# Attention and two expert layers on one core: k's low part in one subtract, rank work behind the last products

## The chip, the cores and the metric

One core of a Trainium2 chip. Times are device microseconds of the whole kernel; lower is better. TensorE (PE in the rows), VectorE (DVE), ScalarE (ACT), GpSimd (POOL) and SyncE (SP, which only issues DMAs) each run their own queue of instructions in order and wait for each other by semaphores.

## The reference

Causal attention with 4 batches of 12 heads, 448 tokens and 64 columns a head, then two mixture-of-experts layers over the 1792 tokens of 768 columns:

```python
scores = scale * np.matmul(q, k.transpose(0, 1, 3, 2))
scores = np.where(mask, -1000000000.0, scores)
attn = softmax(scores)
x = np.matmul(attn, v)
logits = x @ w_gate + modality_bias[modality_id]
e_idx = np.argmax(logits, axis=1)
h = np.maximum(x[mask] @ w1[e], 0.0)
out[mask] = gate_w[mask, None] * (h @ w2[e])
```

The lines on logits, experts and output run twice: the first layer (m1 below) with a modality bias on the logits, the second (m2) without, on the output of the first. There are 8 experts, each with w1 of 768x1024 and w2 of 1024x768. A token goes to one expert.

## The kernel before, in words

Every float32 matrix is split in a high part (type fp32r) and a low part (the rest), and a product is made of three: high by high, high by low, low by high. In m1 the names are `h` and `l` for a weight's high and low part, `xh` and `xl` for the tokens, `hth` and `htl` for the hidden rows. High parts are made by ScalarE (L765 for weights), low parts by VectorE (L769).

**Attention** works on 24 pairs of heads. The string ORDER (L37 to L46) lists the steps of one body, each with an offset that says of which pair; bodies overlap, so one body holds steps of several pairs. `trans` transposes q or k on PE into PSUM, `thi` makes the high part on ScalarE, `tlo` (L113 to L125) the low part on VectorE. Two heads sit in the 128 partitions, 64 each. From pair 1 on a score is two matmuls (L165, L166): the first has q's high and low part of one head stacked in 128 rows against k's high part twice (moved there by DMAs, `mv`), the second k's low part against q's high part. So that the second counts one head alone, k's low part goes into `klz`, a pair of buffers of 128 x 2 x 448 whose other half is zero from the start (L260 to L263): two subtracts, one for each head (L125). `score` (L146 to L166) is in the printed code below.

At each `step` of ORDER the loop over the plan (L300 to L325) pops one function from a list `todo`: the routing of a batch, once the batch's heads are done (`Route1.stages`, L499 to L614; `batch`, L1150). Batch 2, the third, is routed between the heads of the fourth; PW, PL and XW (L328) count empty steps in it. Then m1's first tokens are gathered and transposed. `turn` (L1062) turns the gate's weights for m2 by six transposes into the bank `turned`, two copies to `y` and a DMA, at the head of body 1. WARM (L33) is the count of matmuls on zeros at the start.

**The expert layers** work in blocks of 128 tokens of one expert. `Moe.body` (L950 to L1013) is one block: up products (L832 to L835), the hidden rows to ScalarE, transposes (`htrans`, L858 to L866, which makes `hth` on ScalarE and `htl` on VectorE), down products (L844) into two halves `py[0]` and `py[1]` of 384 columns, each over the first four (KA) and the second four (KB) slices of 128 hidden rows, and the scaling (L881). In `down` a list names the products: "hh" is `h` by `hth`, "lh" is `h` by `htl`, "hl" is `l` by `hth`; those in one list alternate slice by slice. `switch` (L900) loads and splits the next expert's weights where the next block has another. Most blocks run in a device loop (L943 to L948); the one before it is of kind "first", the ones behind it "before" and "last". At the loop's head and end the engines meet.

While m1 runs, the next layer's routing is done for the block before: eight logits of a block on VectorE (L1253, from `y` by `wgb`), `choose` (L671 to L679), `ranks` (L697 and L698 on PE, L699 and L702 on ScalarE) and `rows` (L706 to L725 on VectorE). These hang on hooks of the block: head1 (L1262), up21 (L1269), choose, down1. m2 has the same body without them.

Of the kernel before, what the change touches and what calls it, by code (L numbers as in the profile page):

```python
# [22 lines left out]
E = 8  # L23
FF = 1024
CP = 112
# [7 lines left out]
WARM = 12  # L33
SLOW = 5
# [9 lines left out]
    expo_1_3:1 step expo_1_2:0 thi_q:-1 step ocopy_1:2 ptrans_1_0:1 plo_0_2:1 step score_0_3:0 phi_1_0:1 expo_1_0:0 step  # L44
# [5 lines left out]
def attention(tc, cst, q, k, v, wg1, x1, lg, psh, spare, hooks):  # L50
# [6 lines left out]
    with ExitStack() as c:  # L57
# [54 lines left out]
        def tlo(n, nm):  # L112
            pt, x = pair[n]["pt" + nm], pair[n]["x" + nm]  # L113
            if nm == "q":
                if n == 0:
                    lo = pair[n]["ql"] = spare[:, :S]
                else:
                    lo = pair[n]["ql"] = qk.tile([128, S], F32R, tag="ql", name=f"ql{n}", bufs=1)
                nc.vector.scalar_tensor_tensor(out=lo, in0=pt, scalar=-0.125, in1=x[:, 0], op0=ALU.mult, op1=ALU.subtract)
            else:  # L120

                lo = pair[n]["kl"] = klz[n % 2]
                for j in range(2):
                    r = slice(j * HD, (j + 1) * HD)
                    nc.vector.tensor_tensor(out=lo[r, j], in0=pt[r], in1=x[r, 0], op=ALU.subtract)  # L125
# [16 lines left out]
        def score(n, j, i):  # L142
            s = unit.setdefault((n, j), {})
            r = slice(j * HD, (j + 1) * HD)
            xq, xk, kl = (pair[n][x] for x in ("xq", "xk", "kl"))
            w = (i + 1) * CP  # L146

            o = CP if i == 1 else 0
            key = f"bank{max(i, 1)}"
            if key not in s:  # L150

                sp, tag = [(ps_s, "ps"), (psh, "h0"), (psh, "h1")][scores[0] % 3]
                scores[0] += 1
                s[key] = sp.tile([CP, max(w, 3 * CP)], F32, tag=tag, name=f"ps{n}_{j}_{i}", padded_shape=[CP, 512])
            bank = s[key]
            ps = s["ps", i] = bank[:, o : o + w]
            qs = slice(i * CP, w)
            if n == 0:

                ql = pair[n]["ql"]  # L160
                nc.tensor.matmul(ps, xq[r, 0, qs], xk[r, 0, :w], start=True, stop=False)
                nc.tensor.matmul(ps, ql[r, qs], xk[r, 0, :w], start=False, stop=False)
                nc.tensor.matmul(ps, xq[r, 0, qs], kl[r, j, :w], start=False, stop=True)  # L163
            else:
                nc.tensor.matmul(ps, xq[:, j, qs], xk[:, j, :w], start=True, stop=False)  # L165
                nc.tensor.matmul(ps, xq[:, j, qs], kl[:, j, :w], start=False, stop=True)  # L166
# [50 lines left out]
        def ocopy(n, j):  # L217

            t = unit[n, j]["t"] = sm.tile([128, S], F32, tag="t", name=f"t{n}_{j}", bufs=3)
            nc.scalar.copy(t, unit[n, j]["o"])  # L220
# [16 lines left out]
        def norm(n, g):  # L237
# [4 lines left out]
            l = get(ll, b, sm, [CP, NC, H, E], tag="ll", name=f"ll{b}", bufs=2)  # L242
# [17 lines left out]
        klz = [one.tile([128, 2, S], F32R, name=f"klz{i}") for i in range(2)]  # L260
        for x in klz:
# [4 lines left out]
        for _ in range(WARM):  # L266
            nc.tensor.matmul(warm, idle[:, :128], idle[:, :512], start=True, stop=True)
# [13 lines left out]
        steps = dict(load=load, mv=mv, store=store, splitv=splitv, trans=trans, thi=thi, tlo=tlo, score=score, mini=mini, expo=expo, ptrans=ptrans, phi=phi,  # L281
# [27 lines left out]
        for at, (body, f, n) in enumerate(plan):  # L309
            if body == 1 and plan[at - 1][0] < 1:  # L310
                hooks["turn"](ps_o.tile([128, 512], F32, tag="po", name="turned"))
# [16 lines left out]
PW, PL, XW = 12, 4, 24  # L328
# [149 lines left out]
class Route1:  # L478
# [17 lines left out]
    def stages(self, b, bias, first):  # L496
# [120 lines left out]
        return choice + [self.wait] + rank + slot[:2] + gate[:2] + slot[2:4] + gate[2:4] + slot[4:6] + gate[4:] + slot[6:] + rest  # L617
# [159 lines left out]
class Moe:  # L777
# [173 lines left out]
    def body(self, j, hooks, kind=""):  # L951
# [40 lines left out]
        down(py, 0, KA, ["hh", "lh"])  # L992
# [8 lines left out]
        down(py, 0, KA, ["hl"])  # L1001
        if last:
            down(py, 1, KA, ["hh", "lh"])
# [22 lines left out]
def tile_attention_moe_moe(ctx: ExitStack, tc, q, k, v, mid, wg1, bias, w1a, w2a, wg2, w1b, w2b, out):  # L1026
# [31 lines left out]
    with tc.tile_pool(name="bias", bufs=1) as p:  # L1058
# [3 lines left out]
        def turn(bank):  # L1062

            src = st["hs"][:, : KD * E].rearrange("p (k e) -> p k e", e=E)
            for a, b in ((0, 4), (4, KD)):
# [3 lines left out]
            nc.sync.dma_start(wgt, y[:E])  # L1069
# [192 lines left out]
    def head1(j):  # L1262
        out1(j)
        logits(0, 1, 2, 3, 4, 5)
# [6 lines left out]
    def up21(j):  # L1271
        r2.slots()
        logits(6, 7)
# [25 lines left out]
    with tc.manual_schedule():  # L1299
# [143 lines left out]
```

## Time and profile before

| | |
|---|---|
| median of 3 runs | 953.6 us (952.13 to 954.86) |
| profiled execution | 953.22 us |
| its span in the profile | 950.1 us |
| attention, by the trace | to some 262 us |
| m1's loop | 302.4 to 537.1 us |
| mean granted clock of PE | 0.99 of 2.4 GHz |

The page gives the busy time of each engine, the waits of an engine name who ended them, and the timeline lists the instructions of a stretch, with the idle time before them in brackets. Windows give the busy time of each engine in a stretch and the clock that PE was granted. All times of rows are counted from the start of the span.

### The profile page before, as it was taken

What the parts mean: (1) busy time and instruction counts of PE and PEld (TensorE: products, weight loads), DVE (VectorE), ACT (ScalarE), POOL (GpSimd) and SP (SyncE); (2) the same over time, 40 slices, a digit from 0 to 9 for tenths busy, and PEclk for the clock granted to TensorE, in tenths of its full rate; (3) what the DMA queues carried; (4) which work ended last, traced back from release to release, by engine and by line L of the source; (5) the groups of instructions that cost most, each with busy time, mean ns of one, the idle gap of its engine ahead of it and who ended that gap; (6) DMA issues with size and microseconds to landing.
All of it is one profiled execution on the core that took longest, in us unless ns stands there. A gap on an engine that the chain in (4) does not pass through costs nothing. (4 is left out here: it accounts for less than half of the span.)

```text
span 950.1 us, 21195 instructions
## 1 busy us (share of the span) xinstructions
PE 907.9 (96%) x5432; PEld 804.2 (85%) x5433; DVE 626.6 (66%) x1792; ACT 494.1 (52%) x1137; POOL 170.5 (18%) x225
## 2 busy tenths in 40 slices
PE   7999999999999999988999999999999999999996
PEld 5898898988768898877998788788888888988885
DVE  4999999998566766798767688511176117383743
ACT  4998888888552222271222277212276226573653
POOL 5122414228310000000000000111012102030202
PEclk8999999999999999998999999999999999999999
DMA  6777887766367121245112043540069116295610
GB/s 139 167 184 174 191 194 189 181 167 163 140 219 290 50 66 50 72 166 199 55 61 77 18 171 146 196 171 30 36 227 360 49 33 247 92 344 220 243 48 8
DMA packets 121721, 138.50 MB, mean 146 GB/s; under 512 B 77175, under 2 KB 96759, under 8 KB 121350
## 3 DMA queue, kind: packets, MB, share of 16 engines
q1 hardware_dynamic: 116902, 118.23, 40.9%
q0 software_dynamic: 4768, 19.67, 6.1%
q8 instruction: 22, 0.36, 0.2%
q14 instruction: 29, 0.24, 0.1%
HBM read 117.69 MB, written 24.01 MB: 149 GB/s over the span
## 5 line engine op out<-in xcount | busy, mean ns | idle before, releaser
L769 DVE TENSOR_TENSOR l<-raw,h 128x768 fp32r<-128x768 f32 (+1 forms) x148 | 147.5, 1061 | 12.1 <-ACT h L765 11.9
L765 ACT CAST h<-raw 128x768 fp32r<-128x768 f32 (+1 forms) x154 | 131.2, 925 | 7.5 <-issue 5.4
L866 DVE SCALAR_TENSOR_TENSOR htl<-m2ht,hth 128x512 fp32r<-128x512 f32 x36 | 24.8, 690 | 143.1 <-ACT hth L865 143.1
L1253 DVE CUSTOM_DVE_ANT_0 junk<-y,wgb 128x768 bf16<-128x768 f32 x104 | 99.5, 957 | 14.2 <-ACTq L900 8.6
L178 ACT ACTIVATE P<-ps,m 112x336 f32<-112x336 f32 (+1 forms) x192 | 95.4, 505 | 22.2 <-DVE m L171 21.4
L844 PE MATMUL m2y<-h,hth 128*128 128x384 f32 x272 | 93.1, 342 | 0.0
L171 DVE CUSTOM_DVE_ANT_0 ps<-ps,mask 112x336 f32<-112x336 f32 (+1 forms) x192 | 85.5, 456 | 10.7 <-PE ps L163 4.2
L844 PE MATMUL m2y<-h,htl 128*128 128x384 f32 x272 | 91.6, 337 | 0.0
L832 PE MATMUL m2h<-h,xh 128*128 128x512 f32 x204 | 81.9, 402 | 1.2 <-ACTq L947 1.2
L207 DVE TENSOR_TENSOR ptl<-pp,pth 112x448 fp32r<-112x448 f32 x144 | 77.7, 540 | 6.3 <-ACT pth L201 6.1
L833 PE MATMUL m2h<-h,xl 128*128 128x512 f32 x204 | 80.9, 396 | 0.0
L194 PE MATMUL pp<-cident,P 112*112 112x112 f32 x480 | 71.3, 263 | 5.8 <-DVE ptl L207 5.4
L201 ACT CAST pth<-pp 112x448 fp32r<-112x448 f32 x144 | 67.2, 480 | 10.0 <-PE pp L194 9.5
L844 PE MATMUL m1y<-h,htl 128*128 128x384 f32 x192 | 65.8, 343 | 5.3 <-DVE htl L866 5.3
L844 PE MATMUL m1y<-h,hth 128*128 128x384 f32 x192 | 67.5, 351 | 0.0
L194 PEld LDWEIGHTS pp<-cident,P 112*112 112x112 f32 x480 | 52.0, 134 | 15.5 <-PE ps L166 6.1
L795 POOL DMA_INDIRECT xg<-y_scratch,ic x21 | 21.4, 1018 | 232.4 <-PE m2y L844 148.5
L214 PE MATMUL po<-pth,vs 112*128 112x448 f32 x192 | 62.2, 337 | 0.0
L844 PE MATMUL m2y<-l,hth 128*128 128x384 f32 x272 | 60.3, 343 | 1.1 <-issue 0.4
L165 PE MATMUL ps<-xk,xq 128*112 128x336 f32 (+3 forms) x184 | 60.6, 337 | 0.4 <-ACT P L178 0.2
L795 POOL DMA_INDIRECT xg<-x_scratch,ic x16 | 16.4, 1023 | 248.2 <-PE m1y L844 195.5
L1189 POOL DMA_INDIRECT out_dram<-y,ic x19 | 36.4, 1915 | 124.6 <-ACTq L900 66.4
(459 smaller groups left out, 2192.6 us busy)
## 6 DMA issues: line engine op xcount, KB each, us to landing
raw<-in_moe_w_dram SPq DMA_DIRECT2D x46, 1536.0 KB, 9.7
xk<-xk SPq DMA_DIRECT2D x69, 112.0 KB, 3.5
y_scratch<-y SPq DMA_DIRECT2D x16, 384.0 KB
lk<-in_k_dram SPq DMA_DIRECT2D x48, 112.0 KB, 2.6
lq<-in_q_dram SPq DMA_DIRECT2D x48, 112.0 KB, 3.3
lv<-in_v_dram SPq DMA_DIRECT2D x24, 224.0 KB, 4.5
x_scratch<-xs SPq DMA_DIRECT2D x24, 224.0 KB, 3.0
xq<-ql SPq DMA_DIRECT2D x46, 112.0 KB, 2.7
```

The costliest lines, as they stand in the source:

```text
L171: nc.vector.tensor_tensor_reduce(out=s["ps", i], in0=s["ps", i], in1=mask[:, S - (i + 1) * CP :], scale=1.0, scalar=3.0e38, op0=ALU.add, o ...
L178: nc.scalar.activation(P, s["ps", i], AF.Exp, bias=s["m"][:, i : i + 1], scale=-1.0, accum_out=rs[:, j, i : i + 1])
L194: nc.tensor.transpose(pt[:, at : at + CP], s["P", i][:, kc * CP : (kc + 1) * CP], ident[:CP, :CP])
L201: nc.scalar.copy(h[:, a : a + w], pt)
L207: nc.vector.tensor_tensor(out=l[:, a : a + w], in0=pt, in1=s["pth"][:, a : a + w], op=ALU.subtract)
L214: nc.tensor.matmul(o[:, kc * CP :], vs[:, j, kc, :], s["pth"][:, seg], start=kc == 0, stop=False)
L765: self.nc.scalar.copy(hi[k], raw[:, k, :])
L769: eng.tensor_tensor(out=lo[k], in0=raw[:, k, :], in1=hi[k], op=ALU.subtract)
L832: mm(ph, xh[:, s], W.h1[k][:, f], start=k == 0, stop=False)
L833: mm(ph, xl[:, s], W.h1[k][:, f], start=False, stop=False)
L844: mm(py[n], rows[p[0]][:, s], (W.h2 if p[1] == "h" else W.l2)[k][:, f], start=k == 0 and p == "hh", stop=stop and k == ks[-1] and p == par ...
L1253: vec.tensor_tensor_reduce(out=junk, in0=y, in1=wgb[:, e], scale=1.0, scalar=0.0, op0=ALU.mult, op1=ALU.add, accum_out=r2.lg[:, e : e + 1])
```

## The change

It has five parts.

1. k's low part is one subtract of 128x448 into a plain tile `kl`. The zero-padded pair of buffers is now q's (`qz`): a new step `alone`, after q's high part, copies it there on GpSimd, one copy of 64x448 for each head, from pair 1 on. The second matmul of a score is `kl` by `qz`.
2. The tiles `t` of `ocopy` have two buffers in place of three, `ll` one in place of two.
3. Three more matmuls on zeros (FILLS) come ahead of the transposes of k of pair 1. `turn` is in two parts: four transposes and a copy where all was before, the last two, their copy and the DMA at the 12th step of body 1.
4. PL is 8 in place of 4, XW 28 in place of 24, and three empty steps (RW) in place of one stand ahead of the ranks of batch 2.
5. In blocks of all kinds but "last" the down products go KA high rows, KA low rows, KB high rows, KB low rows, for both halves; the hook "down" with ranks and rows comes behind the two scales. Of the logits three come in head1 and five after `htl` of the first half; in the block before the last two (`upy`) three of them come after the choice of the likeliest expert.

```diff
+FILLS = 3
+TURN = 12
...
-    expo_1_3:1 step expo_1_2:0 thi_q:-1 step ocopy_1:2 ptrans_1_0:1 plo_0_2:1 step score_0_3:0 phi_1_0:1 expo_1_0:0 step
+    expo_1_3:1 step expo_1_2:0 thi_q:-1 alone:-1 step ocopy_1:2 ptrans_1_0:1 plo_0_2:1 step score_0_3:0 phi_1_0:1 expo_1_0:0 step
...
-
-                lo = pair[n]["kl"] = klz[n % 2]
+                lo = pair[n]["kl"] = qk.tile([128, S], F32R, tag="kl", name=f"kl{n}")
+                nc.vector.tensor_tensor(out=lo, in0=pt, in1=x[:, 0], op=ALU.subtract)
+
+        def alone(n):
+
+            if n > 0:
                 for j in range(2):
                     r = slice(j * HD, (j + 1) * HD)
-                    nc.vector.tensor_tensor(out=lo[r, j], in0=pt[r], in1=x[r, 0], op=ALU.subtract)
+                    nc.gpsimd.tensor_copy(qz[n % 2][r, j], pair[n]["xq"][r, 0])
...
-                nc.tensor.matmul(ps, xq[:, j, qs], kl[:, j, :w], start=False, stop=True)
+                nc.tensor.matmul(ps, qz[n % 2][:, j, qs], kl[:, :w], start=False, stop=True)
...
             if body == 1 and plan[at - 1][0] < 1:
-                hooks["turn"](ps_o.tile([128, 512], F32, tag="po", name="turned"))
+                turns = hooks["turn"](ps_o.tile([128, 512], F32, tag="po", name="turned"))
+                turns.pop(0)()
+            elif body == 1 and f == "step" and turns and sum(p[:2] == (1, "step") for p in plan[:at]) == TURN:
+                turns.pop(0)()
+            elif (f, n) == ("trans_k", 1):
+
+                warmth(FILLS)
...
-PW, PL, XW = 12, 4, 24
+PW, PL, RW, XW = 12, 8, 3, 28
...
-        return choice + [self.wait] + rank + slot[:2] + gate[:2] + slot[2:4] + gate[2:4] + slot[4:6] + gate[4:] + slot[6:] + rest
+        return choice + [self.wait] * (RW if b == B - 2 else 1) + rank + slot[:2] + gate[:2] + slot[2:4] + gate[2:4] + slot[4:6] + gate[4:] + slot[6:] + rest
...
-        down(py, 0, KA, ["hh", "lh"])
+
+        down(py, 0, KA, ["hh", "lh"] if last else ["hh", "hl"])
...
-            down(py, 1, KA, ["hh", "lh"])
-            down(py, 1, KA, ["hl"])
-            down(py, 0, KB, ["hh", "lh"])
-            down(py, 0, KB, ["hl"], True)
-            hook("down")
-            down(py, 1, KB, ["hh", "lh"])
-            down(py, 1, KB, ["hl"], True)
+            down(py, 1, KA, ["hh", "hl"])
+            down(py, 0, KA, ["lh"])
+            down(py, 1, KA, ["lh"])
+            down(py, 0, KB, ["hh", "hl"])
+            down(py, 1, KB, ["hh", "hl"])
+            down(py, 0, KB, ["lh"], True)
+            down(py, 1, KB, ["lh"], True)
         for n in range(2):
             self.scale(py, col, n)
+        if not last:
+            hook("down")
...
     def head1(j):
         out1(j)
-        logits(0, 1, 2, 3, 4, 5)
+        logits(0, 1, 2)
...
         r2.slots()
-        logits(6, 7)
+        logits(3, 4, 5, 6, 7)
...
-            logits(6, 7)
+            logits(3, 4)
             r2.most(count("cntz", r2.ohs))
             edv["s"], edv["e"], edv["a"] = r2.e0(ET.SP), r2.e0(ET.DVE), r2.e0(ET.Activation)
+            logits(5, 6, 7)
```

ScalarE at the end of a block of m1's loop, before: the copy of the ranks and the exponential (L699, L702) stand ahead of the two scales (L881).

```order
L699 COPY r2rk<-rk_5289 128x8
L702 REGISTER_ALU
L702 ACTIVATE r2ex,r2se<-r2d 128x8
L881 ISA
L881 ACTIVATE y<-m1y_5104,t1gate 128x384
L881 REGISTER_ALU
L881 ACTIVATE y<-m1y_5105,t1gate 128x384
```

The same with the change:

```order
L897 ISA
L897 ACTIVATE y<-m1y_5150,t1gate 128x384
L897 REGISTER_ALU
L897 ACTIVATE y<-m1y_5151,t1gate 128x384
L715 REGISTER_ALU
L715 COPY r2rk<-rk_5352 128x8
L718 REGISTER_ALU
L718 ACTIVATE r2ex,r2se<-r2d 128x8
```

Copy and exponential now come behind both scales, and the row work on VectorE waits for that copy.

PE at the same place, before: the ranks (`rk`) stand between the first half's last low weights and the second half's twelve KB products, of which the first stand here.

```order
L844 MATMUL m1y_5104<-l_6_4569,hth 128x384
L844 MATMUL m1y_5104<-l_7_4570,hth 128x384
L697 REGISTER_ALU
L697 LDWEIGHTS cones
L697 MATMUL rk_5289<-r2ohs,cones 128x8
L698 REGISTER_ALU
L698 LDWEIGHTS ctri
L698 MATMUL rk_5289<-r2oh,ctri 128x8
L844 MATMUL m1y_5105<-h_4_4559,hth 128x384
L844 MATMUL m1y_5105<-h_4_4559,htl 128x384
```

With the change (m1y_5150 is the first half, m1y_5151 the second):

```order
L860 MATMUL m1y_5151<-h_6_4610,htl 128x384
L860 MATMUL m1y_5151<-h_7_4611,htl 128x384
L713 REGISTER_ALU
L713 LDWEIGHTS cones
L713 MATMUL rk_5352<-r2ohs,cones 128x8
L714 REGISTER_ALU
L714 LDWEIGHTS ctri
L714 MATMUL rk_5352<-r2oh,ctri 128x8
L916 COMPARE_AND_BRANCH
```

The ranks are the block's last matmuls, and the products with `htl` stand just before them.

VectorE in the loop body around `htl` of the first half, before; each logit is an instruction on 128x768 and a read of its sum:

```order
L1253 ISA junk,r2lg<-y,wgb 128x768
L1253 ISA r2lg 128x1
L866 REGISTER_ALU
L866 SCALAR_TENSOR_TENSOR htl<-m1ht_5133,hth 128x512
L1253 REGISTER_ALU
```

With the change, from the third logit to the second one behind `htl`:

```order
L1276 ISA junk,r2lg<-y,wgb 128x768
L1276 ISA r2lg 128x1
L882 REGISTER_ALU
L882 SCALAR_TENSOR_TENSOR htl<-m1ht_5179,hth 128x512
L1276 REGISTER_ALU
L1276 ISA junk,r2lg<-y,wgb 128x768
L1276 ISA r2lg 128x1
```

Before, six logits stand ahead of `htl` and two behind it; with the change three and five. Behind the last logit come, in both, the low parts of the second half of W2 (where the expert changes), the tokens' low parts, `htl` of the second half and `choose`.

## Rows read from the trace of the kernel before

**Rows 1.** The page: span, and busy us (share) xinstructions of each engine.

```profile
span 950.1 us, 21195 instructions
...
PE 907.9 (96%) x5432; PEld 804.2 (85%) x5433; DVE 626.6 (66%) x1792; ACT 494.1 (52%) x1137; POOL 170.5 (18%) x225
```

**Rows 2.** List of waits of PE: waiting line <- who ended it: us, times, longest.

```profile
PE pp L194 <- DVE ptl L207: 5.4, 9, 1.0
PE m1y L844 <- DVE htl L866: 5.3, 1, 5.3
PE turned L1067 <- ACT y L1068: 2.4, 1, 2.4
...
PE pf L235 <- DVE klz L125: 1.5, 5, 0.4
...
PE rk L530 <- DVE klz L125: 1.2, 1, 1.2
```

**Rows 3.** Busy us of each engine by stretch, PE's clock, DMA share, GB/s.

```profile
50.00:75.00 25.00, 25.00 (x217) 23.90 (x215) 24.80 (x86) 23.62 (x75) 5.41 (x8) 1.00 0.74 173
...
sum 175.00, PE 164.23 PEld 150.49 DVE 161.59 ACT 149.06 POOL 64.18; mean PE 23.46 PEld 21.50 DVE 23.08 ACT 21.29 POOL 9.17
```

**Rows 4.** VectorE in attention: durations min/median/max; groups with busy, mean | idle before.

```profile
L125 DVE TENSOR_TENSOR klz<-ptk,xk x48: 602/622/628, 6.9 to 229.0; 64x448 fp32r<-64x448 f32 x48
...
L119 DVE SCALAR_TENSOR_TENSOR ql<-ptq,xq 128x448 fp32r<-128x448 f32 x22 | 13.7, 625 | 0.7
...
L227 DVE RECIPROCAL ri<-ri 112x8 f32<-112x8 f32 x22 | 4.2, 193 | 3.6 <-POOL ri L224 3.6
```

**Rows 5.** GpSimd's groups: a copy in SBUF.

```profile
L277 POOL COPY mov<-cident 64x768 f32<-64x768 f32 x2 | 1.6, 819 | 0.1
```

**Rows 6.** Timeline of the start: start us, us, engine, line [idle before].

```profile
14.96 0.41 PE L1067 MATMUL turned<-cident,hs 128*8 128x128 f32 x2 [2.42 <-ACT y L1068]
```

**Rows 7.** Stretches of 2 us: PE's clock is the number before DMA share.

```profile
16.00:18.00 2.00, 2.00 (x8) 1.27 (x8) 0.57 (x2) 0.84 (x4) 1.92 (x3) 0.50 0.34 70
...
428.00:430.00 2.00, 0.00 (x0) 0.00 (x0) 1.97 (x5) 0.00 (x0) 0.00 (x0) 0.55 0.61 197
430.00:432.00 2.00, 1.60 (x5) 1.60 (x6) 1.97 (x4) 0.00 (x0) 0.00 (x0) 0.50 0.43 52
...
434.00:436.00 2.00, 2.00 (x10) 2.00 (x9) 2.00 (x3) 0.55 (x1) 0.00 (x0) 0.75 0.93 376
```

**Rows 8.** Timeline at the entry of m1's loop.

```profile
299.22 0.17 DVE L706 TENSOR_TENSOR r2jk<-r2rk,r2oh 128x8 f32<-128x8 f32 x1 [2.83 <-ACT r2rk L699]
...
301.19 0.58 ACT L881 ACTIVATE y<-m1y1f,t1gate 128x384 f32<-128x384 f32 x1 [1.33 <-PE m1y1f L844]
301.20 0.16 DVE L725 TENSOR_TENSOR r2ohs<-r2ohs,r2oh 128x8 bf16<-128x8 bf16 x1
...
302.38 0.47 PE L832 MATMUL m1h<-h,xh 128*128 128x512 f32 x1 [1.23 <-ACTq L947]
```

**Rows 9.** Timeline at the exit of m1's loop.

```profile
535.57 0.58 ACT L881 ACTIVATE y<-m1y,t1gate 128x384 f32<-128x384 f32 x1 [1.20 <-PE m1y L844]
535.80 0.16 DVE L725 TENSOR_TENSOR r2ohs<-r2ohs,r2oh 128x8 bf16<-128x8 bf16 x1
...
537.06 0.47 PE L832 MATMUL m1h0b<-h,xh 128*128 128x512 f32 x1 [1.60 <-PEq L1438]
```

**Rows 10.** Timeline of the block with a new expert, VectorE and PE.

```profile
411.44 6.91 DVE L769 TENSOR_TENSOR l<-raw,h 128x1024 fp32r<-128x1024 f32 x6 [0.74 <-ACT h L765]
...
423.78 0.95 DVE L1253 CUSTOM_DVE_ANT_0 junk<-y,wgb 128x768 bf16<-128x768 f32 x1
...
429.66 0.69 DVE L866 SCALAR_TENSOR_TENSOR htl<-m1ht,hth 128x512 fp32r<-128x512 f32 x1
...
432.15 3.56 DVE L769 TENSOR_TENSOR l<-raw,h 128x768 fp32r<-128x768 f32 x4
...
430.40 0.69 PE L844 MATMUL m1y<-h,htl 128*128 128x384 f32 x1 [5.26 <-DVE htl L866]
```

More of the change, by code (lines that the diff above doesn't have):

```diff
@@ L162, in score @@
                 nc.tensor.matmul(ps, ql[r, qs], xk[r, 0, :w], start=False, stop=False)
-                nc.tensor.matmul(ps, xq[r, 0, qs], kl[r, j, :w], start=False, stop=True)
+                nc.tensor.matmul(ps, xq[r, 0, qs], kl[r, :w], start=False, stop=True)
             else:
                 nc.tensor.matmul(ps, xq[:, j, qs], xk[:, j, :w], start=True, stop=False)
-                nc.tensor.matmul(ps, xq[:, j, qs], kl[:, j, :w], start=False, stop=True)
+                nc.tensor.matmul(ps, qz[n % 2][:, j, qs], kl[:, :w], start=False, stop=True)
         def mini(n, j, i):
@@ L217, in ocopy @@
         def ocopy(n, j):
-            t = unit[n, j]["t"] = sm.tile([128, S], F32, tag="t", name=f"t{n}_{j}", bufs=3)
+            t = unit[n, j]["t"] = sm.tile([128, S], F32, tag="t", name=f"t{n}_{j}", bufs=2)
             nc.scalar.copy(t, unit[n, j]["o"])
@@ L241, in norm @@
             xs = get(s, "xs", xp, [CP, NC, 128], tag="xs", name=f"xs{n}", bufs=1)
-            l = get(ll, b, sm, [CP, NC, H, E], tag="ll", name=f"ll{b}", bufs=2)
+            l = get(ll, b, sm, [CP, NC, H, E], tag="ll", name=f"ll{b}", bufs=1)
             rg = s["ri"][:, :, 2 * g : 2 * g + 2].rearrange("p j c -> p c j").unsqueeze(3)
@@ L259, in attention @@
         nc.vector.memset(mask, 0.0)
-        klz = [one.tile([128, 2, S], F32R, name=f"klz{i}") for i in range(2)]
-        for x in klz:
+        qz = [one.tile([128, 2, S], F32R, name=f"qz{i}") for i in range(2)]
+        for x in qz:
             for j in range(2):
@@ L265, in attention, with warmth @@
         warm = ps_o.tile([128, 512], F32, tag="po", name="warm")
-        for _ in range(WARM):
-            nc.tensor.matmul(warm, idle[:, :128], idle[:, :512], start=True, stop=True)
+        def warmth(times):
+            for _ in range(times):
+                nc.tensor.matmul(warm, idle[:, :128], idle[:, :512], start=True, stop=True)
+        warmth(WARM)
         for n, nms in ((0, "kq"), (1, "kq"), (0, "v"), (1, "v")):
@@ L280, in attention @@
         hooks["start"]()
-        steps = dict(load=load, mv=mv, store=store, splitv=splitv, trans=trans, thi=thi, tlo=tlo, score=score, mini=mini, expo=expo, ptrans=ptrans, phi=phi,
+        steps = dict(load=load, mv=mv, alone=alone, store=store, splitv=splitv, trans=trans, thi=thi, tlo=tlo, score=score, mini=mini, expo=expo, ptrans=ptrans, phi=phi,
                      plo=plo, pv=pv, ocopy=ocopy, ria=ria, ri=ri, final=final, norm=norm)
@@ L1000, in body @@
         hook("w1")
-        down(py, 0, KA, ["hl"])
         if last:
+            down(py, 0, KA, ["hl"])
             down(py, 1, KA, ["hh", "lh"])
@@ L1064, in turn, with part @@
             src = st["hs"][:, : KD * E].rearrange("p (k e) -> p k e", e=E)
-            for a, b in ((0, 4), (4, KD)):
+            def part(a, b):
                 for k in range(a, b):
@@ L1068, in turn @@
                 nc.scalar.copy(y[:E, a * 128 : b * 128], bank[:E, : (b - a) * 128])
-            nc.sync.dma_start(wgt, y[:E])
+                if b == KD:
+                    nc.sync.dma_start(wgt, y[:E])
+            return [lambda: part(0, 4), lambda: part(4, KD)]
         def start():
```

## The prediction

> **What bounds the kernel now.** I read the page's busy table first. TensorE (PE) works 907.9 us of the 950.1 us span, 96% [rows 1]: a saving can only come from the 42 us in which PE stands, or from a stretch at the lower of its two clocks (1.2 in place of 2.4 GHz, in the rows 0.50 in place of 1.00). The profiled execution took 953.22 us, 0.4 under the median of the three runs, 953.6; my sum is made against 953.2.
>
> Second comes the list of what PE waits for [rows 2]. Its first entry is VectorE's (DVE's) subtraction of the probabilities, 5.4 us in nine waits; the second is a single wait of 5.3 us for `htl`, in the first expert layer (m1). The wait for the gate's transposed weights (`turned`) is 2.4 us, and the two lines in which PE stands behind the `klz` subtract give 1.5 and 1.2 us.
>
> Third, the stages. From 50 to 75 us, with no routing work, PE is busy 25.00 us of 25: nothing can be had there from VectorE, though VectorE itself is at 24.80. From 75 to 250 us, where the routing of the batches lies between the heads, PE is busy 164.23 of 175 us [rows 3], so some 10.8 us stand open, and VectorE is what it waits for most. After that the two expert layers run at PE's pace, with three holes that matter here: at the entry of m1's loop, at its exit, and in the one block where the expert changes.
>
> **The attention, part by part.** VectorE now makes k's low part in two subtracts of 64x448, 622 ns each in the median. They become one of 128x448; the subtract of that form for q takes 625 ns [rows 4]. That is 0.62 us less VectorE work a pair, in 24 pairs 14.9 us. What it is worth is not 14.9 but what PE waits: in the ten pairs between 75 and 250 us, where PE has idle time behind VectorE, I take the full 0.62 each, 6.2 us. The floor is half, 3, if ScalarE's casts take over the wait (they are late next); the ceiling is the waits on `ptl` and `klz` together, 8.1 us [rows 2]. In the other pairs, some thirteen, I take 0.5 in all, since PE is full there.
>
> In exchange GpSimd (POOL) makes two copies of 64x448 for 23 pairs. The trace has no such copy; the nearest row is 64x768 in 819 ns [rows 5], by its width 0.48 us, and at most 0.82. That is 1 to 1.6 us a pair. GpSimd has 170.5 us of work in all [rows 1], so the copies fit in its gaps; the scores that read them come several steps later. I cost them at nothing in the middle of the attention. If that cover goes, a score waits up to 1 us a pair.
>
> At the start, the last two transposes and their copy and the DMA behind them move from the head of pair 1 to twelve steps later. The idle time of 2.42 us before them [rows 6] goes; two transposes of 0.4 us come back later. Three warm products fill the hole before the transposes of k of pair 1. PE ran at 0.50 from 16 to 22 us, and was busy 2.00 of 2.00 in each 2 us of it [rows 7], while VectorE had only 0.57 in the first of the three: three microseconds of work were lost to the clock. If the holes before are gone and the clock holds, the gain is 2.0 + 3.0 = 5.0; if it falls all the same, 2. I take 4.0, because VectorE is the next to be full after 22 us.
>
> At the end, the ranks of the third batch come three steps later and what follows (gather, first transposes of the tokens) about ten. GpSimd's queue there now holds the last copies ahead of the sums that VectorE inverts; VectorE already stood 3.6 us in all before that reciprocal [rows 4]. The copies are 1 us in front of the chain and the gather is less hidden: I take 1.5 us lost, from 0 to 3. Buffers cut from three to two and two to one add no wait that I can find in the order: the reader of the old tile is past before the next writer comes.
>
> Sum for the attention: -4.0 - 6.2 - 0.5 + 1.5 = -9.2, from -14 to -5.
>
> **The loop blocks, part by part.** The number of products is the same. Those with the low weights (`l`) come earlier, those with h's low rows (`htl`) later. In a plain block both are ready long before, so it costs nothing. What moves is the rank work: on PE it stood twelve products before the block's end, now it is behind the last; on ScalarE it is behind both scales; VectorE's row work starts after that. Within the loop the next block's products cover it. At the two ends of the loop nothing does.
>
> Entry of the loop [rows 8]: the row work took VectorE from 299.22 to 301.36, 2.14 us, and ScalarE's last scale ended at 301.77; PE started the loop at 302.38, 0.6 later, having stood 1.23 us. Now rows start after the scale and the copy of the ranks, near 302.0, end at 304.2, and the loop is entered at some 304.5 to 304.8: +2.1, if the loop's first products wait for VectorE to arrive, as they do for ScalarE. If they do not, +0.5, the copy and the exponential on ScalarE.
>
> Exit [rows 9]: the last scale ended at 536.15 and the row work at 535.96; PE started again at 537.06, 1.60 after its last product. Here all engines meet. Now ranks at 536.2, rows 536.4 to 538.7, PE at 539.8: +2.7, from 2 to 3.
>
> The block with the new expert [rows 10]: PE stood 5.26 us for `htl`, which on VectorE came after six logits. Now only three stand before it, so `htl` comes 3 us earlier. But VectorE does the other five right after, and then the four low parts of W2's second half (3.56 us, from 432.15), and the products with these are no longer behind all products with `h`: they come at once. Re-timed with the same durations: W1's lows (6.91 us) start 1.1 later, because the choice waits behind the logits; rows, W2's first lows, three logits, `htl` at 428.9, five logits to 433.8, W2's second lows ready at 434.7, 435.6, 436.5, 437.4. PE gets to the first of them at 430.5 and goes at their pace to 437.4. Then 16 products remain, 2.8 us at full clock: the block ends at 440.5, or 442.3 at half, and it ended at 441.6. So the stall moves and +0.3 is the middle, -1.1 to +1.5.
>
> The clock. In this block PE stood 5.26 us and the granted clock fell to 0.50 while it stood; from 428 to 436 the windows show 0.55, 0.50, 0.50 and 0.75 [rows 7]. Of that PE lost 0.8 + 1.0 + 0.5 = 2.3 us while busy; had it worked all the time, 0.9 + 1.0 + 1.0 + 0.5 = 3.4. After the change PE stands 3.3 us at the entry and 4.3 at the exit, where it stood 1.23 and 1.60 at clock 1.00. The first is longer than the 2.42 of the start, the second near 5.26. I take one fall for the two, 2.7 us; ends 0 and 6. By the Trainium skill, "TensorE: Matmul & The Clock Gate", section "What you observe" and the table below it, the clock falls to 1.2 GHz after PE was idle and comes back only after sustained work; the trace agrees at 428 and at 16 us. By that rule both holes cost, which is the second rival below.
>
> The second expert layer has the new order of products but no rank work: 0. Sum for the blocks: 2.1 + 2.7 + 0.3 + 2.7 = +7.8, from 1.4 to 12.6.
>
> **Together:** 953.2 - 9.2 + 7.8 = 951.8; from 953.2 - 14 + 1.4 to 953.2 - 5 + 12.6, that is 941 to 961 if every end met; the ends are independent, so about 946 to 957 is likely.
>
> **The rivals.**
> *The loop's ends are cheap* (faster). PE does not wait for VectorE at the entry and the clock holds at both places: the blocks cost 0.5 + 2.0 + 0.3 = 2.8 in place of 7.8, the attention stays -9.2: 946.8, and down to 944 where the attention gives more. For it: the wait at the entry is put down to ScalarE alone [rows 8]. Against it: at the exit all engines must be through.
>
> *The clock falls at both ends* (slower). The mechanism is the row work behind the scales; the place is the loop's entry and exit; the price is two falls at 3.4, with 4.8 of standing and 1.5 in the changed block: 13.1. With -9.2 from the attention that is 957.1, slower than before. It decides from the point where the attention gives less than 9.8. For it: PE goes straight into dense products after each hole, so a whole stretch at 0.50 counts. Against it: the hole of 1.6 at clock 1.00 did no harm, and nothing in the trace lies between 2.42 and 5.26.
>
> *The copies hold VectorE* (slower). If each GpSimd copy kept VectorE from working for its 0.48 us, a pair would have 0.96 - 0.62 = 0.34 us more in place of less. Ten routed pairs and thirteen plain ones, whose VectorE is at 24.80 of 25 [rows 3], would lose up to 8 us where I count a gain of 6.7: 953.2 - 4.0 + 7.8 + 1.5 + 7.8 = 966.3. The Trainium skill has the rule, in "SBUF — State Buffer", section "Who interferes with whom": VectorE with two SBUF inputs contends with a GpSimd instruction that reads SBUF, with one such input it does not. VectorE's operations here read PSUM and one SBUF tile, and the 48 subtracts of k lie between 602 and 628 ns all through the attention, whatever GpSimd did beside them [rows 4]: nothing there was held for the length of a copy, so I give this little.
>
> *The stall only changes its name.* In the changed block the wait for `htl` becomes a wait for the W2 lows; that is in my sum already.
>
> **How the numbers follow.** A measurement of this kernel tells about 0.3%, 2.9 us, from no change. I give my case 45%, the cheap ends 31%, two falls of the clock 18%, the copies 4%, 2% for what I have not seen. My case's own spread is 948 to 956: a third of it (0.14) is under 950.7, the rest (0.27) within, 0.04 above 956.5. The cheap ends are faster in 0.28 of 0.31. Two falls: 0.08 within, 0.10 slower. With the rest: faster 0.42, same 0.38, slower 0.20. The range that leaves out 2 in 10 is 945.5 to 957.5.
>
> **What would show it.** The waits on `klz` gone and those on `ptl` shorter; PE from 75 to 250 us about 6 us shorter; clock 1.00 from 15 to 22 us. At the loop's entry and exit, row work beginning after the last scale, with PE standing 3.3 and 4.3 us, and the clock at 0.50 after at least one. In the changed block PE's wait on `l`, no longer on `htl`, with nearly the same end. I would be wrong if the attention gives under 5 or over 14 us, or if plain blocks no longer take the same time.

## The result, and the profile after

The change makes the kernel slower: 964.98 us (median of 4 runs, 964.45 to 969.11) against 953.77 beside it, a ratio of 1.0128 with a 95% interval of 1.011 to 1.0146. The forecast was 951.8, with a range from 945.5 to 957.5. The profiled execution took 969.11 us with a span of 967.4, 17.3 over the span of before, so the trace shows some 4 us more than the median run; its mean granted clock is 0.977, in the other three runs 0.980 to 0.984, against 0.991 before.

The page and the list of PE's waits answer to [rows 1, 2]:

```profile
span 967.4 us, 21611 instructions
...
PE 918.9 (95%) x5435; PEld 814.4 (84%) x5436; DVE 614.8 (64%) x1768; ACT 490.2 (51%) x1137; POOL 195.8 (20%) x271
```

```profile
PE pp L200 <- DVE ptl L213: 6.3, 7, 1.9
PE m1h0b L848 <- PEq L1462: 4.1, 1, 4.1
PE pf L241 <- DVE kl L124: 3.8, 2, 2.6
PE m1y L860 <- DVE l L785: 2.5, 4, 1.7
...
PE m1h L849 <- DVEq L963: 1.9, 1, 1.9
```

VectorE has 11.8 us less to do, as intended (626.6 before), and GpSimd 25.3 us more. `turned` is gone from the list, and in the block with a new expert the wait of the products for `htl` has become one for `l`. But PE stands longer behind `kl` and `ptl` than it did behind `klz` and `ptl`, and there are long stands at the entry of m1's loop (m1h, VectorE) and behind it (m1h0b).

The same stretch as in [rows 3], and then the places where PE was granted half its clock (the number before the DMA share):

```profile
sum 175.00, PE 162.42 PEld 152.53 DVE 148.37 ACT 141.86 POOL 80.22; mean PE 23.20 PEld 21.79 DVE 21.20 ACT 20.27 POOL 11.46
```

```profile
204.00:214.00 10.00, 10.00 (x53) 9.21 (x53) 6.63 (x30) 4.91 (x15) 0.69 (x3) 0.51 0.25 59
221.00:227.00 6.00, 6.00 (x31) 5.77 (x30) 4.03 (x12) 4.35 (x11) 5.87 (x5) 0.50 0.57 138
244.00:252.00 8.00, 7.78 (x40) 7.41 (x40) 4.91 (x17) 4.82 (x18) 0.08 (x1) 0.57 0.10 40
313.00:316.00 3.00, 3.00 (x9) 2.33 (x8) 2.48 (x6) 0.00 (x0) 0.00 (x0) 0.50 0.39 131
549.00:558.00 9.00, 6.19 (x14) 4.45 (x15) 2.90 (x6) 0.00 (x0) 0.00 (x0) 0.50 0.13 47
```

Before, the clock was low near 16 and 430 us alone. Now it holds at 430, is still low near 16 us, and falls five times elsewhere: three times in the routing of the third batch, once at each end of m1's loop.

Set side by side by PE's first instruction of each stage, the 17.3 us come about so. At 198.6 us, in the last pairs, the changed kernel is 4.3 us ahead. By m1's first products into `m1y0f` it is 6.7 behind: the third batch's stretch lost 11.0. The entry of the loop costs 3.8, the loop gives 0.3 back, its exit costs 2.5 as a stand and 4.4 more in the next products, m1's last block 1.4, and the rest gives 1.2 back.

Where the 11.0 us begin, in the timeline of the changed kernel, GpSimd first and then VectorE and PE:

```profile
199.26 1.17 POOL L131 CAST qz<-xq 64x448 fp32r<-64x448 f32 x2
200.51 0.24 POOL L535 TENSOR_TENSOR r1d<-lg,r1mx 112x32 f32<-112x32 f32 x1
200.69 0.61 POOL L97 CAST vs<-lv 112x512 fp32r<-112x512 f32 x1
201.38 1.26 POOL L98 TENSOR_TENSOR vs<-lv,vs 112x512 fp32r<-112x512 f32 x1
```

```profile
200.78 0.57 DVE L536 SCALAR_TENSOR_TENSOR r1wt<-r1d,crank 112x32 f32<-112x32 f32 x1 [1.00 <-POOL r1d L535]
201.38 0.19 DVE L538 TENSOR_REDUCE r1m<-r1wt 112x4 f32<-112x32 f32 x1
201.60 1.09 DVE L539 TENSOR_TENSOR r1oh<-r1wt,r1m 112x32 bf16<-112x32 f32 x1
202.61 0.61 DVE L124 TENSOR_TENSOR kl<-ptk,xk 128x448 fp32r<-128x448 f32 x1
```

```profile
203.28 1.05 PE L241 MATMUL pf<-mov,t 128*112 128x72 f32 x5 [2.63 <-DVE kl L124]
```

And the kernel before, at the same steps:

```profile
204.17 0.19 DVE L520 SCALAR_TENSOR_TENSOR r1wt<-r1d,crank 112x32 f32<-112x32 f32 x1
204.39 0.18 DVE L522 TENSOR_REDUCE r1m<-r1wt 112x4 f32<-112x32 f32 x1
204.61 0.19 DVE L523 TENSOR_TENSOR r1oh<-r1wt,r1m 112x32 bf16<-112x32 f32 x1
204.72 1.25 DVE L125 TENSOR_TENSOR klz<-ptk,xk 64x448 fp32r<-64x448 f32 x2
```

Two things happen. The copies of q (`qz`) stand in GpSimd's queue ahead of `r1d`, for which VectorE then waits 1.00 us. And two of VectorE's small steps, `r1wt` and `r1oh`, take 0.57 and 1.09 us in place of 0.19 and 0.19, while GpSimd splits v (`vs`) beside them; each of them ends 0.05 us after the GpSimd instruction beside it (201.35 after 201.30, 202.69 after 202.64). `kl`, which follows in VectorE's queue, comes late; PE stands 2.63 us for the products behind it, and its clock falls. At 217 us VectorE stands 1.62 us for `r1rsi`, behind the next copies, and at 227, 237 and 241 us 2.15, 2.51 and 1.98 us for `ri`, `y` and `ri`; what stands ahead of these three in GpSimd's queue is not copies but low parts of weights, the splits of v and routing work.

The two ends of the loop, against [rows 8, 9]:

```profile
307.79 0.58 ACT L897 ACTIVATE y<-m1y1f,t1gate 128x384 f32<-128x384 f32 x1
308.26 0.16 ACT L715 COPY r2rk<-rk 128x8 f32<-128x8 f32 x1
```

```profile
308.46 0.17 DVE L722 TENSOR_TENSOR r2jk<-r2rk,r2oh 128x8 f32<-128x8 f32 x1 [5.34 <-ACT r2rk L715]
...
310.79 0.15 DVE L741 TENSOR_TENSOR r2ohs<-r2ohs,r2oh 128x8 bf16<-128x8 bf16 x1
```

```profile
309.24 0.47 PE L848 MATMUL m1h<-h,xh 128*128 128x512 f32 x1 [1.44 <-ACTq L963]
311.56 0.50 PE L849 MATMUL m1h<-h,xl 128*128 128x512 f32 x1 [1.85 <-DVEq L963]
...
549.75 0.76 PE L848 MATMUL m1h0b<-h,xh 128*128 128x512 f32 x1 [4.10 <-PEq L1462]
```

The row work begins behind the scale and the copy. One product enters the loop when ScalarE has arrived, and the next one waits 1.85 us for VectorE: 3.29 us of standing together. At the exit PE stands 4.10.

### The profile page after: what moved, and what is told of

The parts are those of the page before. It is cut to its first block, busy times and chain, and to the rows that moved or that the text cites. A ratio compares the mean times of both kernels' runs of the same rounds, so it can differ in the third digit from the quotient of the medians.

```text
span 967.4 us, 21611 instructions
## 1 busy us (share of the span) xinstructions
PE 918.9 (95%) x5435; PEld 814.4 (84%) x5436; DVE 614.8 (64%) x1768; ACT 490.2 (51%) x1137; POOL 195.8 (20%) x271
## 5 line engine op out<-in xcount | busy, mean ns | idle before, releaser
L860 PE MATMUL m2y<-l,hth 128*128 128x384 f32 x272 | 91.5, 336 | 0.0
L200 PE MATMUL pp<-cident,P 112*112 112x112 f32 x480 | 74.5, 271 | 6.5 <-DVE ptl L213 6.3
L860 PE MATMUL m1y<-l,hth 128*128 128x384 f32 x192 | 65.2, 340 | 2.5 <-DVE l L785 2.5
L200 PEld LDWEIGHTS pp<-cident,P 112*112 112x112 f32 x480 | 55.6, 140 | 14.1 <-DVE ptl L213 3.8
L848 PE MATMUL m1h<-h,xh 128*128 128x512 f32 x144 | 58.7, 407 | 1.9 <-ACTq L963 1.4
```

What stands on the lines that cost most here:

```text
L200: nc.tensor.transpose(pt[:, at : at + CP], s["P", i][:, kc * CP : (kc + 1) * CP], ident[:CP, :CP])
L848: mm(ph, xh[:, s], W.h1[k][:, f], start=k == 0, stop=False)
L860: mm(py[n], rows[p[0]][:, s], (W.h2 if p[1] == "h" else W.l2)[k][:, f], start=k == 0 and p == "hh", stop=stop and k == ks[-1] and p == par ...
```

## The experiments

Three theories. **Q**: in the third batch VectorE is held by GpSimd, in its queue and beside it, and PE's clock falls after each stand. **W**: the later steps (part 4) alone make that loss. **R**: the row work behind the scales holds PE at both ends of m1's loop. Ratios below are to the kernel before on the same chip; the changed kernel's is 1.0128.

### x1: the old steps

```diff
-PW, PL, RW, XW = 12, 8, 3, 28
+PW, PL, RW, XW = 12, 4, 1, 24
```

> The changed kernel with PL, RW and XW as before (4, 1, 24). Theory Q (GpSimd's queue: in the third batch VectorE waits for small GpSimd sums that stand behind the copies of q and behind later routing work, and PE's clock falls after each stand): the two stands of PE behind kl near 200 and 217 us stay, for the copies still stand ahead of r1d; the stands near 237 and 241 us, behind y and ri, go: 3 us and one fall of the clock, about 960. Theory W (the later steps alone make the loss): all five stands go and the attention ends 11 us earlier: about 954.

Measured: 967.23 us, 1.0145 (1.0108 to 1.0181). PE stands 1.51 and 1.15 us behind `kl`, and 4.03 us near 235. Theory W fails, and so does my 960: undoing part 4 alone gives nothing. Its VectorE at the choice of the third batch:

```profile
200.31 0.19 DVE L536 SCALAR_TENSOR_TENSOR r1wt<-r1d,crank 112x32 f32<-112x32 f32 x1 [1.00 <-POOL r1d L535]
...
200.76 0.19 DVE L539 TENSOR_TENSOR r1oh<-r1wt,r1m 112x32 bf16<-112x32 f32 x1
```

The wait for `r1d` is the same 1.00 us, the copies being where they were. But `r1wt` and `r1oh` are at 0.19 us again: with one empty step the split of v no longer runs beside them.

### x2: two subtracts, no copies

```diff
-                lo = pair[n]["kl"] = qk.tile([128, S], F32R, tag="kl", name=f"kl{n}")
-                nc.vector.tensor_tensor(out=lo, in0=pt, in1=x[:, 0], op=ALU.subtract)
...
+                lo = pair[n]["kl"] = klz[n % 2]
                 for j in range(2):
                     r = slice(j * HD, (j + 1) * HD)
-                    nc.gpsimd.tensor_copy(qz[n % 2][r, j], pair[n]["xq"][r, 0])
+                    nc.vector.tensor_tensor(out=lo[r, j], in0=pt[r], in1=x[r, 0], op=ALU.subtract)
...
-                nc.tensor.matmul(ps, qz[n % 2][:, j, qs], kl[:, :w], start=False, stop=True)
+                nc.tensor.matmul(ps, xq[:, j, qs], kl[:, j, :w], start=False, stop=True)
```

> The changed kernel with k's low part as before (two 64x448 subtracts into a padded buffer, no copies on GpSimd). Theory Q: the waits of VectorE for r1d and r1rsi shrink to those of before, PE's stands of 2.6 and 1.2 us behind kl and their two falls of the clock go, about 9 us; the 4 to 6 us that one subtract had gained are lost: about 960 to 962, with clock 1.00 from 200 to 230 us. Theory W: the stands remain and the gain is lost: 969 or more.

Measured: 964.53 us, 1.0111 (1.0074 to 1.0147). Without copies `r1d` comes at once, yet PE still stands 2.33 us behind `klz`:

```profile
205.26 0.57 DVE L531 SCALAR_TENSOR_TENSOR r1wt<-r1d,crank 112x32 f32<-112x32 f32 x1
...
206.08 1.09 DVE L534 TENSOR_TENSOR r1oh<-r1wt,r1m 112x32 bf16<-112x32 f32 x1
207.10 1.25 DVE L126 TENSOR_TENSOR klz<-ptk,xk 64x448 fp32r<-64x448 f32 x2
```

`r1wt` and `r1oh` are as slow as in the change, beside GpSimd's cast and subtract of v (205.17 to 207.12). So the queue is only half of it: the split of v, which the three empty steps put beside these two operations, holds them, and then the two subtracts cost their 0.6 us more. My theory Q had the queue alone; the second half was formed here.

### x4: the copies four steps later

```diff
-    expo_1_3:1 step expo_1_2:0 thi_q:-1 alone:-1 step ocopy_1:2 ptrans_1_0:1 plo_0_2:1 step score_0_3:0 phi_1_0:1 expo_1_0:0 step
-    mv_k_1:-1 score_0_1:0 step expo_1_1:0 tlo_k:-1 step ptrans_0_1:1 tlo_q:-1 mini_0_3:0 phi_0_1:1 step expo_0_3:0
+    expo_1_3:1 step expo_1_2:0 thi_q:-1 step ocopy_1:2 ptrans_1_0:1 plo_0_2:1 step score_0_3:0 phi_1_0:1 expo_1_0:0 step
+    mv_k_1:-1 score_0_1:0 step expo_1_1:0 tlo_k:-1 step ptrans_0_1:1 tlo_q:-1 alone:-1 mini_0_3:0 phi_0_1:1 step expo_0_3:0
```

> The changed kernel with GpSimd's two copies for a pair four steps later in the order, behind q's low part. Theory Q: r1d now stands ahead of the copies, VectorE gets it about 1 us earlier; PE's stand at 200 us falls from 2.6 to 1 or less and the clock holds there: 5 to 6 us, about 959. The stand at 217 us may move. Theory W: no change, 965.

Measured: 957.87 us, 1.0058 (1.0037 to 1.0078): 0.7% better by the place of 46 copies. The split of v now stands behind the copies and comes after `r1oh`:

```profile
194.98 0.51 DVE L536 SCALAR_TENSOR_TENSOR r1wt<-r1d,crank 112x32 f32<-112x32 f32 x1
...
195.75 0.35 DVE L539 TENSOR_TENSOR r1oh<-r1wt,r1m 112x32 bf16<-112x32 f32 x1
```

```profile
196.70 1.01 PE L241 MATMUL pf<-mov,t 128*112 128x72 f32 x8 [0.90 <-DVE kl L124]
```

PE stands 0.90 us in place of 2.63, and the clock holds there; it still falls at 219 us, behind a stand of 2.48. Theory Q, with both halves: this edit moves the copies behind `r1d` and the split of v behind `r1oh` at once, and does not say how much each is worth.

x2 and x4 differ in more than k's low part, since x2 still has the slow `r1oh` and the stand behind it. What one subtract is worth shows ahead of the third batch, between q's high part of the fifth pair and that of the 22nd, first before, then in the change, then in x4:

```profile
39.54 0.54 ACT L108 ACTIVATE xq<-ptq 128x448 fp32r<-128x448 f32 x1
202.93 0.55 ACT L108 ACTIVATE xq<-ptq 128x448 fp32r<-128x448 f32 x1
```

```profile
37.83 0.54 ACT L110 ACTIVATE xq<-ptq 128x448 fp32r<-128x448 f32 x1
198.64 0.55 ACT L110 ACTIVATE xq<-ptq 128x448 fp32r<-128x448 f32 x1
```

```profile
35.85 0.55 ACT L110 ACTIVATE xq<-ptq 128x448 fp32r<-128x448 f32 x1
193.79 0.55 ACT L110 ACTIVATE xq<-ptq 128x448 fp32r<-128x448 f32 x1
```

That is 163.39, 160.81 and 157.94 us: 5.5 us gained in x4, 2.6 in the change. So the copies in their first place cost 2.9 us before the third batch is reached. There VectorE stands 0.47 us for `r1d` in each of the first two batches and 0.48 us for one `ri`; in x4, and before, no wait for GpSimd there is over 0.25 us.

### x3 and x7: the ranks ahead of the last eight products

```diff
             down(py, 1, KB, ["hh", "hl"])
+            hook("down")
             down(py, 0, KB, ["lh"], True)
...
-        if not last:
-            hook("down")
```

> The changed kernel with ranks and rows put ahead of the last eight products of a block instead of behind the scales. If the row work behind the scales holds PE at both ends of m1's loop: PE's stand at the entry falls from 3.3 to about 1.3 us, at the exit from 4.1 to about 1.6, both falls of the clock there go: 4.5 + 5 = 9 us, about 956. If the falls come from something else (the order of the products): only 4.5 us, about 960.5.

Measured: 961.02 us, 1.0091 (1.0063 to 1.0119), 3.5 us for a forecast of 9. At the entry PE stands 1.23 and 0.16 us and the clock stays at 1.00. At the exit it still stands 2.37, the clock still falls, and then 2.94 us follow in which it waits for nothing that the trace shows.

With the copies four steps later as well (x7):

> The changed kernel with both: copies of q four steps later and ranks ahead of the last eight products. If the two losses (GpSimd's queue in the third batch, row work at the loop's ends) are independent, their gains add: 1.0128 - 0.007 - 0.004 = 1.002 of the time before. If the clock falls that were avoided by one come back through the other: 1.005.

Measured: 954.96 us, 1.002 (1.0002 to 1.0038): the two add, 0.0038 for the ranks here and 0.0037 in x3.

### x5: the old blocks

Part 5 undone: order of products, ranks and logits as before, of which this is the core.

```diff
-            down(py, 0, KB, ["hh", "hl"])
-            down(py, 1, KB, ["hh", "hl"])
-            down(py, 0, KB, ["lh"], True)
-            down(py, 1, KB, ["lh"], True)
+            down(py, 0, KB, ["hh", "lh"])
+            down(py, 0, KB, ["hl"], True)
+            hook("down")
+            down(py, 1, KB, ["hh", "lh"])
+            down(py, 1, KB, ["hl"], True)
...
-        logits(0, 1, 2)
+        logits(0, 1, 2, 3, 4, 5)
```

> The changed kernel with part 5 undone: order of down products, ranks and logits as before. If the ends of m1's loop and the last block of m1 cost what the trace of the change shows there (entry +3.8, exit +6.9, last block +1.4, changed block -0.3): 10 to 12 us come back, but the clock falls of the attention stay, about 1.004 of the time before. If only the standing counts and the clock would fall somewhere anyway: 5 us, about 1.008.

Measured: 955.6 us, 1.0034 (1.0015 to 1.0053), 9 us better. That is more than the ranks' 3.5, so the blocks have another loss.

### x8 and x9: copies later and old blocks, with the old and the new steps

x9 has the edits of x4 and x5; x8 has that of x1 besides:

```diff
-PW, PL, RW, XW = 12, 8, 3, 28
+PW, PL, RW, XW = 12, 4, 1, 24
```

> The changed kernel with copies four steps later, and PL, RW, XW and the blocks as before: what is left is one subtract with copies, the start and the smaller pools. If the forecast of the attention was right but for the place of the copies: 7 to 9 us faster than before, 0.991 to 0.993. If the copies hold VectorE everywhere: no gain, 1.000 or more.

Measured: 950.35 us, 0.9972 (0.9951 to 0.9993).

> As the run before it, but with PL, RW and XW of the change (8, 3, 28). If three empty steps ahead of the ranks put v's split on GpSimd beside VectorE's choice and lengthen it, and the later values make VectorE wait for GpSimd at 215 and 232 us: 4 to 6 us slower than with the old steps, 0.997 to 0.999. If the steps are harmless: the same as it.

Measured: 948.75 us, 0.9954 (0.9937 to 0.9971). Both are faster than the kernel before. x8 gains some 3 us where 7 to 9 were expected if only the place of the copies was wrong, so that place was not all. x9 was expected 4 to 6 us slower than x8 and is not: the new steps are no loss once the copies stand right. What is left of theory Q shows in x9, in VectorE's timeline and in GpSimd's ahead of the first of these two waits:

```profile
217.51 0.20 DVE L233 RECIPROCAL ri<-ri 112x8 f32<-112x8 f32 x1 [3.25 <-POOL ri L230]
...
233.16 0.20 DVE L233 RECIPROCAL ri<-ri 112x8 f32<-112x8 f32 x1 [1.98 <-POOL ri L230]
```

```profile
212.99 2.39 POOL L785 TENSOR_TENSOR l<-raw,h 128x1024 fp32r<-128x1024 f32 x1
215.32 1.83 POOL L595 TENSOR_TENSOR htl<-hs,r1vals 112x448 fp32r<-112x448 f32 x2
```

VectorE stands 3.25 and 1.98 us for a sum of 112x8, which waits on GpSimd behind a weight's low part and routing work, not behind copies; PE stands 2.49 and 1.03 us behind it and the clock is low from 220 to 230 us.

### y1: the old start

x9 with part 3 undone:

```diff
-FILLS = 3
+FILLS = 0
...
                 turns.pop(0)()
+                turns.pop(0)()
```

> The kernel with copies four steps later and the old blocks (run x9, 0.9954 of the time before), with part 3 undone as well: no extra warm products and all six transposes for turned at the head of body 1. If the start is worth what was forecast: 4 us slower than x9, 0.9996. By the traces of the change, where the first pair's later steps came 1.7 to 3.6 us earlier and the clock still fell near 16 us in most runs: 2 us slower, 0.9975. If it is worth nothing: 0.9954.

Measured: 948.28 us, 0.9953 (0.9936 to 0.997), as x9. Part 3 is worth nothing that these runs can tell.

### y2 and y3: order of products, and logits, one at a time

y2 is x9 with the new order of products and ranks ahead of the last eight (x3's place); y3 is x9 with three and five logits:

```diff
-        logits(0, 1, 2, 3, 4, 5)
+        logits(0, 1, 2)
...
-        logits(6, 7)
+        logits(3, 4, 5, 6, 7)
```

> x9 with the new order of the down products, ranks ahead of the last eight, and the logits as before. If what the new blocks still cost with early ranks (1.002 against 0.9954 for x9) comes from the products with htl at the end, which hold W2's high parts longer and so the new expert's weights and htl of m1's last block: 1.001, with a stand of 1.9 to 2.7 us at htl in m1's last block. If it comes from the split of the logits: 0.996.

Measured: 952.75 us, 0.9998 (0.9981 to 1.0016), with a stand of 2.33 us at `htl` in m1's last block.

> x9 with the logits three and five instead of six and two, and the products as before. If the split is harmless or helps (htl 3 us earlier in the block with a new expert): 0.992 to 0.9954. In the old order of products the W2 lows are needed later than htl, but htl of the second half comes 1.8 us later behind the five logits: then PE's stand moves there and the time stays 0.9954. If the split is what costs: 1.001.

Measured: 957.26 us, 1.0047 (1.0028 to 1.0066). Every block of m1's loop now takes 19.2 us in place of 18.77: `htl` of the second half comes behind five logits, and in the old order it is needed early. The waits of PE in this kernel, from 303 to 540 us:

```profile
PE m1y L860 <- DVE htl L882: 9.1, 13, 3.6
```

So the logits need the new order of products; together, in the changed kernel, a block takes 18.75 us. y2 alone agreed with its first expectation, but its reason did not hold:

### z1 and z2: VectorE's program shifted by 24 instructions

In y2's last block VectorE stands between two operations, and the DMA engines are full:

```profile
565.46 0.17 DVE L1316 COPY r2lg<-lgy 128x8 f32<-128x8 f32 x1
571.49 3.56 DVE L785 TENSOR_TENSOR l<-raw,h 128x768 fp32r<-128x768 f32 x4 [5.86 <-ACT hth L881]
```

```profile
q1 hardware_dynamic: 821, 2.54, 97.2%
q14 instruction: 1, 0.01, 0.3%
```

The cast named as releaser (`hth`, done at 571.0) is not what the subtract reads: the casts of `h` were done at 567.9, and in the run below the same subtract starts ahead of that `hth`. VectorE's sequencer had not come to the subtract's wait: from 565.88 on it has no record until a branch at 571.30, 5.4 us. In that time one packet of instructions arrives. The shift adds 24 memsets of a small tile at the start:

```diff
         warmth(WARM)
+        pad = one.tile([1, 8], F32, name="pad")
+        for _ in range(24):
+            nc.vector.memset(pad, 0.0)
```

> The run with the new order of products, early ranks and old logits (y2, 0.9998), with 24 memsets of one small tile added on VectorE in its idle time at the start, so that everything behind them stands 24 instructions later in VectorE's program. Nothing computed changes. If the 5.4 us in which VectorE stood in m1's last block, between two instructions that waited for nothing, came from instructions that were loaded late: the stand moves or goes, 4 us back, 0.9955. If the new order of products makes it: 0.9998 and the same stand.

Measured: 947.29 us, 0.993 (0.991 to 0.9949): the stand is gone, and 6.5 us with it, for work that was only added. In the traces the last block's down products, to m2's first product, take 9.0 us in place of 13.2, which is what was expected; where the rest of the 6.5 comes from is open.

> The changed kernel itself (1.0128) with the same 24 memsets. If VectorE's stand of 3.6 us in m1's last block comes from late instructions: it moves or goes, 1 to 4 us back, 1.009 to 1.012; the stands at the loop's ends and in the third batch stay as they are. If it belongs to the order: 1.0128.

Measured: 964.99 us, 1.0129 (1.0097 to 1.016). In its trace the stand in the last block is gone too, but the median does not move: that loss was 1.4 us in the changed kernel, less than the spread of these runs (961.75 to 970.09).

### y4 and z3: the small sum on VectorE

```diff
-            nc.gpsimd.tensor_scalar(out=r, in0=pair[n]["rs"], scalar1=1e-9, scalar2=None, op0=ALU.add)
+            (nc.vector if n >= 20 else nc.gpsimd).tensor_scalar(out=r, in0=pair[n]["rs"], scalar1=1e-9, scalar2=None, op0=ALU.add)
```

> x9 with the small sum ahead of the reciprocal (ri) on VectorE instead of GpSimd for the last four pairs. If VectorE stands 3.25 and 1.98 us because that sum waits in GpSimd's queue behind the routing work, and PE's clock falls after it: PE's stands of 2.5 and 1.0 us near 217 and 234 us and the fall of the clock from 220 to 230 us go, 3.5 + 3 = 6 us: 0.989. If VectorE then waits for something else at the same place: the same as x9.

Measured: 945.05 us, 0.9906 (0.9884 to 0.9927). It has the lowest median of all, 0.9% under the kernel before: x9 and this one line. Its trace is of the slowest of its four runs (951.07 us; the others 942.82 to 945.98), and shows PE standing 1.00 us where it stood 2.49, with later stands of 1.86 and 2.15 us:

```profile
218.30 0.40 PE L200 MATMUL pp<-cident,P 112*112 112x112 f32 x2 [1.00 <-DVE ptl L213]
```

> The changed kernel with all parts kept and three edits: copies of q four steps later, ranks ahead of the last eight products, the sum ahead of the reciprocal on VectorE for the last four pairs. If the gains add as they did by twos: 1.002 for the first two, less 0.0048 for the third: 0.997. If the clock's falls move elsewhere: 1.002.

Measured: 951.83 us, 0.9975 (0.9957 to 0.9992). The change with all its parts and three edits is a little faster than the kernel before: 15 us lie between it and the change as it was, in the place of 46 copies, of two matmuls a block and of four sums.

## Why the prediction was wrong, by its own steps

x5 parts the miss: with the old blocks, the attention as changed is 0.34% slower than before, some 3 us, where 9.2 us less was forecast. The blocks cost the other 9 us, where 7.8 was forecast. So the attention is where the sum failed.

**One subtract in place of two** was right in size: 6.2 forecast, 5.5 in x4. In the change itself it came to 2.6, because the copies took the rest.

**"I cost them at nothing in the middle of the attention"** is the step that failed. I held GpSimd's 170.5 us of work against the whole span and found gaps for the copies. In the third batch its queue is a link of VectorE's chain: `r1d`, `r1rsi`, `ri` and `y` are small, but VectorE waits for each. I had listed [rows 4] the reciprocal's wait of 3.6 us and put 1.5 on the end; the third batch's stretch lost 11.0 us in the profiled run, and the place of the copies alone is worth 6.7 us of the whole time (x4). The copies' own length, 0.56 us, was within the estimate of 0.48 to 0.82; it was what waits behind them that had been left out.

**The rival of the copies** was given 4%, for VectorE's operations "read PSUM and one SBUF tile". That is true of attention's: the subtract of k takes 0.61 us in the median in the change, so the rival's mechanism is not what happened, and its sum, 966.3, lies near the measured time by luck. `r1wt` and `r1oh` read two SBUF tiles, and I had not looked at them: 0.19 us each grew to 0.57 and 1.09. The Trainium skill, "SBUF — State Buffer", section "Who interferes with whom", has just this: VectorE with two inputs in SBUF contends with a GpSimd instruction that reads SBUF. The traces agree: `kl`, with one such input, takes 0.61 us in x4 too, where GpSimd splits v from 196.13 on, and is not held. The kernel before had already shown such a hold, in the routing of its second batch, where `r1wt` takes 0.78 us and ends with GpSimd's subtract:

```profile
145.38 1.27 POOL L96 TENSOR_TENSOR vs<-lv,vs 112x512 fp32r<-112x512 f32 x1
145.91 0.78 DVE L520 SCALAR_TENSOR_TENSOR r1wt<-r1d,crank 112x32 f32<-112x32 f32 x1
```

But what held them in the third batch was less the copy than the split of v, which part 4 had moved.

**The start** was taken at 4.0 and is worth 0 (y1). The stand of 2.42 us goes, but PE then stands for loads and for VectorE near 13 us (1.79 in the change), and the clock still falls near 16 us in most traces.

**The ends of the loop** were right as stands: 3.3 and 4.3 forecast, 3.29 and 4.10 measured. Of the clock I took one fall for two; both came in the profiled run (313 to 316 and 549 to 558 us). That is the second rival's mechanism. Ranks ahead of the last eight products give 3.5 us back; the stand at the exit then still is 2.37 us, and not 1.60.

**The changed block** was right: +0.3 forecast, -0.2 measured (26.3 us in place of 26.5); the wait of 5.26 us goes, and PE stands 1.74 us for `l` and 1.47 in the transposes, behind `htl`.

**The smaller pools** (part 2) were undone in no run. ScalarE's waits at `t` for PE's products are 4.1 us in all in both traces, so nothing shows a cost there.

**Not foreseen** was m1's last block, 1.4 us here and about 4 in six of the variants. z1 shows that it goes when VectorE's program is shifted; that the instructions were late because of the weights' DMA is what the packet's time suggests, and was not shown. The like stand of PE behind the loop's exit (2.06 us, no releaser) was not tried.

## What to carry to other kernels

Spare time of an engine over the whole span says nothing of a place where another engine waits for its small results: read that engine's queue where the chain is densest, and put bulk work behind the links. A dense engine that stands for two or three microseconds may lose as much again to its clock, so count stands by where they fall, not by their sum. A change that moves code can gain or lose some microseconds by where its instructions come to stand in the program (z1: 6.5); one shift of the program tells this from the change's own effect.

## What the runs showed of the hardware

VectorE's 112x32 step with two SBUF inputs took 1.09 us beside GpSimd's subtract of v (1.26 us) and 0.19 without; with the copy beside it it took 0.35. In the traces of before, of the change, x2 and x4, every such step that was held ended 0.04 to 0.06 us after the GpSimd instruction beside it, whether that was a cast, a copy or a subtract.

VectorE's sequencer stood 5.4 us (y2) at a place where it waits for no engine, while the hardware queue's packets took 97.2% of the DMA engines' time; with 24 instructions more ahead of it, it did not.

PE's stands of 2.3 to 2.7 us in the third batch were followed by a clock of 0.50 within 3 us of their end in every trace that has one, twelve of them, in x2 from the end of the stand on; one of 2.1 us in x8 and those of 0.9 us in x4 and x9 were not; at the loop's exit a stand of 2.3 to 2.4 us was followed by a fall in x3, x7 and y2, and by none in z1 and z3. Falls came behind shorter stands too: 2.0 us after one of 1.05 us in x8, and in x2 at 147 us right behind one of 0.86. So the length of one stand does not tell by itself whether the clock falls.
